# FNet mixing and a gated feed-forward block on one core: fold parts and first-stage groups moved to a regular grid of steps

## The chip, the cores and the metric

The kernel runs on one NeuronCore of one Trainium2 chip. The metric is the device time of one execution in microseconds (us). The engines are named as in the profile: PE (TensorE matmul), PEld (its weight loads), DVE (VectorE), ACT (ScalarE), POOL (GpSimd) and SP (SyncE, which here issues most DMAs).

## What is computed

A two-dimensional Fourier transform of every batch, of which the real part is kept, and then two matrix products with the quick form of GELU between them, all in float32:

```python
# x (8, 3008, 256); moe_w_in (256, 2048); moe_w_out (2048, 256)
X = np.fft.fft(x, axis=1)
X = np.fft.fft(X, axis=2)
x = X.real.astype(np.float32).reshape(B * S, D)      # (24064, 256)
h = x @ w_in
g = h * (1.0 / (1.0 + np.exp(-1.702 * h)))
out = (g @ w_out).astype(np.float32)
```

## The kernel before

**Stages.** The sequence of 3008 positions is split as 47 x 64. A batch goes through five pieces of work:

1. *Load and fold.* `turn` (L189) copies half of the batch, in reversed order, to the DRAM tensor `Xr`; `load_x` (L199, four calls) loads `x` and `Xr` into the one SBUF tile `xt`. `fold1` (L210) then adds and subtracts mirrored columns in `xt` in place. It is called 16 times per batch, for chunk c = 0 to 7 and part 0 or 1, and runs on POOL. Part 0 is a small and a large add (L225 on 111x4, L227 on 111x510 elements), part 1 an add and a subtract (L230, L231, 111x254 each). The very first part (c = 0, part 0) has three more operations that make the tile `e` (L218 to L220).
2. *First-stage groups.* `mix1` (L233, four calls, m = 0 to 3) multiplies `xt` by the tables `w1` on PE (L255). Group m needs the four parts of chunks 2m and 2m+1. The group m = 0 has a few matmuls more, those of `e`. ACT copies the results back to `xt` (`mixed`, L263).
3. *Spill, fill, rotate.* `spill` (L337, two calls per group) writes a group's result to the DRAM tensor `Td`, `fill` (L342, three calls per batch) reads it back in another layout into the tile `t`, and `rotate` (L347) corrects one column by a small matmul and a copy.
4. *Second stage.* `stage2` (L354), once per block of 512 columns, multiplies on PE (L365) and transposes on DVE (L372) into the tile `pq`. `nyquist_out` and `nyquist` (L387, L375) send one row of it through DRAM and load it to all partitions as `nb`.
5. *Feed-forward steps.* The rest of the work, by far the most of it, in 384 steps t.

**Steps.** A step t stands for (batch b, block, half hh, p): eight batches of three blocks of two halves of p = 0 to 7, so 48 steps a batch; `t0 = 48 * b` is a batch's first step. Below, "step k of batch b" is t = 48b + k, and k modulo 8 is p. In each step PE multiplies for the hidden layer (`begin`, into the banks `x`), ACT applies GELU (`forward`, L600, one instruction per step; `activate_back`, L607; both around `backward`, L604, on DVE), and the results are combined by a Strassen-like scheme so that fewer products are needed: `sums` on POOL (L615, L616) and on DVE (L622, L623, at every second step), and one level further down `deeper` on DVE (L646, L648 for part 0, L650 for part 1). The second matrix product, `product` (L697) and `small_products` (L660, PE rows at L684), runs three steps behind (`LAG`). Where it starts a new half, the step is an "opening": k modulo 8 is 3.

At the end of a half DVE also has to combine the eight results: L757 and L758 in p = 2 steps, four times L786 (`combine_small`) in p = 3, L768 and L804 in p = 4, and a transpose L737 (`turned`), from which `store` sends the output, in each of the p = 5 and p = 6 steps.

**How the next batch's first stage is placed.** The order on every engine is written out by hand: the loop over t (L992) calls the work of step t in a fixed order, and at its end all functions that `at(t, fn, ...)` (L935) has noted for that step (`extra`). So a fold part of step k stands on POOL behind the two sums of step k, and a group stands on PE behind all matmuls of its step. The loop over b (L960) notes for each batch, in terms of t0, at which steps the next batch's fold parts, groups, spills (one step after their group), fills, rotate and the loads of the batch after next are issued. The steps of folds and groups are a row of `PLANS` (L932): the first is used for b = 0, the second for b = 1, the third for b = 2 to 6. Negative entries are steps of the batch before. Steps of the kind "group or stage2" are `special`: they use other banks, and `middle` (L578) for the step after next is issued a step later.

`paced(t)` (L391) is a four-byte DMA that reads an element which `forward(t)` writes. It stands on SP's queue just ahead of a large transfer and so keeps that transfer from being issued before step t.

Of the kernel before, what the change touches and what calls it, by code (L numbers as in the profile page):

```python
# [112 lines left out]
def kernel(ctx: ExitStack, tc, x, w_in, w_out, tab1, tab2, out):  # L113
# [800 lines left out]
    for h0 in (0, 512):  # L914
# [14 lines left out]
    finish_out(0)  # L929

    extra, early = {}, {}
    PLANS = ((range(11, 27), (16, 20, 25, 28)), ((-1, 0, 1, 1, 2, 7, 7, 9, 10, 15, 15, 16, 16, 17, 17, 18), (7, 15, 19, 23)),  # L932
             ((-9, -7, -7, -6, -1, 0, 1, 1, 2, 7, 9, 10, 15, 16, 17, 17), (-1, 7, 15, 23)))

    def at(t, fn, *args):  # L935
        extra.setdefault(t, []).append((fn, args))
# [22 lines left out]
        at(7 + i, small_weights, i)  # L959
    for b in range(B):  # L960
        t0 = b * NBLK * NF
        late = 0 if b else 5
        if b + 2 < B:
            for k in range(3):
                at(t0 + 11 + k, paced, t0 + 11 + k)
                at(t0 + 11 + k, turn, b + 2, k)
        if b + 1 < B:
            folds, groups = PLANS[min(b, 2)]
            for c in range(NCH):
                for part in range(2):  # L970
                    at(t0 + folds[2 * c + part], fold1, b + 1, c, part, nc.gpsimd)
                if c % 2:
                    k = t0 + groups[c // 2]
                    at(k, mix1, b + 1, c // 2)
                    for half in range(2):
                        at(k + 1, spill, b + 1, half, c // 2)
            for blk in range(NBLK):
                at(t0 + 27 + blk + late, paced, t0 + 27 + blk + late)
                at(t0 + 27 + blk + late, fill, b + 1, 4 * blk, 4 * blk + 4)
            if b + 2 < B:  # L980
                for k in range(4):
                    at(t0 + 31 + 2 * k + late, paced, t0 + 31 + 2 * k + late)
                    at(t0 + 31 + 2 * k + late, load_x, b + 2, k)
            at(t0 + 36 + 3 * (late > 0), rotate, b + 1)
        for blk in range(NBLK):
            nxt = (b, blk + 1) if blk + 1 < NBLK else (b + 1, 0)
            if nxt[0] < B:
                at(t0 + blk * NF + 8, stage2, *nxt)
                at(t0 + blk * NF + 9, nyquist_out, *nxt)
                at(t0 + blk * NF + 10, nyquist, *nxt)  # L990
# [123 lines left out]
```

## Time and profile before

| | us |
|---|---|
| median of 3 runs | 1857.74 (1855.88 to 1861.3) |
| profiled execution | 1856.81 |
| its span, first to last instruction | 1855.0 |
| PE busy | 1835.9 (99%) |
| DVE busy | 1486.4 (80%) |
| ACT busy | 1148.7 (62%) |
| POOL busy | 995.9 (54%) |

The steps can be told apart by the L600 rows on ACT, one for each step from t = 8 on. From the first L600 row of one batch to that of the next it takes 227.18 us in batch 1, 225.01, 225.03, 225.03 and 225.09 us in batches 2 to 5 and 222.96 us in batch 6. Batch 7 has no next batch, so it issues no folds and no groups.

The DMA engines are busy for 10 to 40% of most slices; the chain that ended last runs along PE for 87% of the span. The page's line of granted clocks shows 9 (90% or more) in all 40 slices, and the core's mean is 1.000.

The busiest lines of POOL are the sums (L616 397.3 us, L615 351.2 us); L227, the large add of a fold, is issued 56 times and takes 1266 ns at least, 1272 ns in the median and 2224 ns at most.

### The profile page before, as it was taken

To read this page: it belongs to the slowest core of one execution; us is meant where nothing else is said; L and a number is where in the kernel's file an instruction comes from. 1 tells how busy PE (TensorE), PEld (TensorE's weight loads), DVE (VectorE), ACT (ScalarE), POOL (GpSimd) and SP (SyncE) were. 2 spreads that over 40 slices of the span, in tenths; PEclk is the share of its full clock that TensorE was granted. 3 is DMA by queue.
4 is the path that set the end of the run, shared out by engine and by line. 5 is a ranking of instruction groups with operands and counts; after the bars stand their busy time and mean duration, and the time that the engine had idled before them with its cause. 6 is when DMAs were issued, how large, how long until landed. Compare 5 with 4: busy or idle time off the path is not lost.

```text
span 1855.0 us, 55973 instructions
## 1 busy us (share of the span) xinstructions
PE 1835.9 (99%) x23722; PEld 1401.5 (76%) x23722; DVE 1486.4 (80%) x1928; ACT 1148.7 (62%) x2241; POOL 995.9 (54%) x1053
## 2 busy tenths in 40 slices
PE   8999999999999999999999999999999999999998
PEld 4677777777777777777777777777777777778776
DVE  6978778878788778887888778877888788878875
ACT  5656666665666666666565666666665666656563
POOL 4786456745655446463655546555465544444442
PEclk9999999999999999999999999999999999999999
DMA  8721331225111341213312132131411111100111
GB/s 275 186 61 34 85 67 28 64 51 99 27 40 44 78 77 21 60 33 90 57 21 66 35 86 52 23 74 31 103 31 31 36 37 36 30 19 13 23 19 24
DMA packets 149706, 105.31 MB, mean 57 GB/s; under 512 B 106057, under 2 KB 130665, under 8 KB 148896
## 3 DMA queue, kind: packets, MB, share of 16 engines
q1 hardware_dynamic: 146624, 99.68, 23.7%
q8 instruction: 187, 3.06, 0.7%
q10 hardware_dynamic: 2832, 2.05, 0.5%
q14 instruction: 63, 0.52, 0.1%
HBM read 64.41 MB, written 48.05 MB: 61 GB/s over the span
## 4 chain that ended last, share of the span: by engine, by line
PE 87%; DVE 8%; DMA 2%; ACT 1%; issue 1%; POOL 0%; DVEq 0%; SPq 0%; ACTq 0%; POOLq 0%
PE x L184 32%; PE o L184 25%; PE low L684 23%; PE o L684 4%; PE ps L255 2%; PE ps L365 1%; DVE big L622 1%; DVE big L650 1%; DVE big L604 1%; DVE big L786 1%; DVE big L646 1%; DMA xt<-in_x_dram 1%; DMA Td<-big 1%; DVE big L804 0%; DVE big L648 0%
## 5 line engine op out<-in xcount | busy, mean ns | idle before, releaser
L615 POOL TENSOR_TENSOR big<-big 128x256 f32<-128x256 f32 (+1 forms) x376 | 351.2, 934 | 804.8 <-ACT big L607 745.4
L184 PE MATMUL x<-pq,wcs 128*64 128x256 f32 (+1 forms) x6016 | 769.0, 376 | 1.1 <-ACT g L597 0.2
L184 PE MATMUL o<-big,wo 128*64 128x256 f32 (+1 forms) x4800 | 620.8, 375 | 0.1
L184 PEld LDWEIGHTS x<-pq,wcs 128*64 128x64 f32 x6016 | 413.8, 137 | 182.7 <-issue 15.3
L597 ACT ACTIVATE g<-x 128x512 f32<-128x512 f32 (+1 forms) x376 | 221.7, 590 | 384.2 <-PE x L184 383.0
L184 PEld LDWEIGHTS o<-big,wo 128*64 128x64 f32 x4800 | 341.3, 137 | 147.7 <-DVE big L622 0.5
L604 DVE TENSOR_TENSOR big<-g,x 128x512 f32<-128x512 f32 (+1 forms) x376 | 250.8, 667 | 190.8 <-ACT big L600 190.6
L616 POOL TENSOR_TENSOR big<-big 128x256 f32<-128x256 f32 (+1 forms) x376 | 397.3, 1057 | 0.0
L585 ACT ACTIVATE x<-nb,af 128x256 f32<-128x256 f32 (+1 forms) x752 | 352.9, 469 | 68.8 <-DVE pq L372 55.7
L684 PE MATMUL low<-big 128*64 128x128 f32 (+1 forms) x5888 | 381.8, 270 | 0.0
L684 PEld LDWEIGHTS low<-big 128*64 128x64 f32 x5888 | 337.0, 137 | 28.7
L600 ACT ACTIVATE big<-x 128x512 f32<-128x512 f32 (+1 forms) x376 | 219.2, 583 | 123.6 <-PE x L184 105.2
L646 DVE TENSOR_TENSOR big<-big 128x1024 f32<-128x1024 f32 (+1 forms) x184 | 235.6, 1280 | 66.2 <-PE low L684 42.4
L607 ACT ACTIVATE big<-big 128x512 f32<-128x512 f32 (+1 forms) x376 | 231.6, 616 | 37.9 <-DVE big L604 35.7
L684 PE MATMUL low<-big,wo 128*64 128x128 f32 (+1 forms) x2944 | 220.6, 271 | 5.9 <-DVE big L650 5.9
L648 DVE TENSOR_TENSOR big<-big 128x512 f32<-128x512 f32 (+1 forms) x184 | 178.7, 971 | 16.3 <-PE x L184 0.5
L684 PEld LDWEIGHTS low<-big,wo 128*64 128x64 f32 x2944 | 171.5, 137 | 11.1 <-DVE big L650 7.7
L650 DVE TENSOR_TENSOR big<-big 128x512 f32<-128x512 f32 (+1 forms) x184 | 172.8, 939 | 0.0
L623 DVE TENSOR_TENSOR big<-big 128x512 f32<-128x512 f32 (+1 forms) x188 | 147.8, 786 | 6.5
L622 DVE TENSOR_TENSOR big<-big 128x512 f32<-128x512 f32 (+1 forms) x188 | 139.5, 742 | 3.3 <-POOL big L615 3.3
L786 DVE TENSOR_TENSOR big<-big,low 128x512 f32<-128x512 f32 (+3 forms) x184 | 109.0, 609 | 3.5
L684 PEld LDWEIGHTS o<-big,wo 128*64 128x64 f32 x1472 | 92.2, 137 | 25.0
(97 smaller groups left out, 1147.2 us busy)
## 6 DMA issues: line engine op xcount, KB each, us to landing
out_dram<-os SPq DMA_DIRECT2D x284, 64.0 KB
t<-Td SPq DMA_DIRECT2D x22, 512.0 KB
Td<-xt SPq DMA_DIRECT2D x56, 192.0 KB
xt<-in_x_dram SPq DMA_DIRECT2D x14, 512.0 KB
xt<-Xr SPq DMA_DIRECT2D x14, 512.0 KB
nb<-Nd SPq DMA_DIRECT2D x23, 256.0 KB
out_dram<-os SPq DMA_DIRECT2D x96, 56.0 KB
Xr<-in_x_dram SPq DMA_DIRECT2D x7, 752.0 KB
```

The costliest lines, as they stand in the source:

```text
L184: nc.tensor.matmul(out[c0:c0 + 64], lhsT=lhs[:, c0:c0 + 64], rhs=rhs, skip_group_check=True, **how)
L585: nc.scalar.activation(x[:, i * 256:i * 256 + n], nbt[b, blk][:, hh * 256:hh * 256 + n], ACTF.Copy, scale=af1[:, f:f + 1])
L597: nc.scalar.activation(two(g[:], n), two(xb[t][:], n), ACTF.Copy, scale=2.0)
L600: nc.scalar.activation(front(t), two(xb[t][:], width(t)), ACTF.Gelu_apprx_sigmoid)
L604: nc.vector.tensor_tensor(back(t), two(gt.pop(t)[:], n), two(xb.pop(t)[:], n), op=ALU.subtract)
L607: nc.scalar.activation(back(t), back(t), ACTF.Gelu_apprx_sigmoid)
L615: eng.tensor_tensor(right(t, S1, n), left(t, A21, n), right(t, A22, n), op=ALU.add)
L616: eng.tensor_tensor(left(t, S3, n), left(t, A11, n), left(t, A21, n), op=ALU.subtract)
L646: nc.vector.tensor_tensor(free(big[:], SUM, *both_), free(big[:], from11 + w, *twice), free(big[:], from11, [at_right(t, 0) + w - from11, ...
L648: nc.vector.tensor_tensor(s2, a11, s1, op=ALU.subtract)
L650: nc.vector.tensor_tensor(s4, a12, s2, op=ALU.subtract)
L684: nc.tensor.matmul(o, lhsT=lhs, rhs=rhs, start=first_in, stop=(p == NP - 2), skip_group_check=True)
```

## The change

The change touches only the placing in steps. It replaces the three rows of `PLANS` by two. The first (b = 0) is as before. The second, now for all b from 1 on, issues one fold part in each of the steps -1, 0, 1, 2, then 7 to 10, 15 to 18 and 23 to 26, and the groups at steps 7, 15, 23 and 31. Before, b = 1 had its parts at -1, 0, 1, 1, 2, 7, 7, 9, 10, 15, 15, 16, 16, 17, 17, 18 and its groups at 7, 15, 19, 23; b = 2 to 6 had them at -9, -7, -7, -6, -1, 0, 1, 1, 2, 7, 9, 10, 15, 16, 17, 17 and at -1, 7, 15, 23.

What follows the groups moves too, for b from 1 on: the fills from steps 27, 28, 29 to 33, 34, 35, the loads of the batch after next from 31, 33, 35, 37 to 36, 38, 40, 42, and rotate from 36 to 39. For b = 0 these stay at 32 to 34, at 36, 38, 40, 42 and at 39.

```diff
-    PLANS = ((range(11, 27), (16, 20, 25, 28)), ((-1, 0, 1, 1, 2, 7, 7, 9, 10, 15, 15, 16, 16, 17, 17, 18), (7, 15, 19, 23)),
-             ((-9, -7, -7, -6, -1, 0, 1, 1, 2, 7, 9, 10, 15, 16, 17, 17), (-1, 7, 15, 23)))
+    PLANS = ((range(11, 27), (16, 20, 25, 28), 32), ([g + k for g in (0, 8, 16, 24) for k in range(-1, 3)], (7, 15, 23, 31), 33))
...
-        late = 0 if b else 5
...
-            folds, groups = PLANS[min(b, 2)]
+            folds, groups, filled = PLANS[min(b, 1)]
...
-                at(t0 + 27 + blk + late, paced, t0 + 27 + blk + late)
-                at(t0 + 27 + blk + late, fill, b + 1, 4 * blk, 4 * blk + 4)
+                at(t0 + filled + blk, paced, t0 + filled + blk)
+                at(t0 + filled + blk, fill, b + 1, 4 * blk, 4 * blk + 4)
...
-                    at(t0 + 31 + 2 * k + late, paced, t0 + 31 + 2 * k + late)
-                    at(t0 + 31 + 2 * k + late, load_x, b + 2, k)
-            at(t0 + 36 + 3 * (late > 0), rotate, b + 1)
+                    at(t0 + 36 + 2 * k, paced, t0 + 36 + 2 * k)
+                    at(t0 + 36 + 2 * k, load_x, b + 2, k)
+            at(t0 + 39, rotate, b + 1)
```

## The prediction, made before the changed kernel was run

> **What bounds the kernel now.** I read the page first (busy shares, chain), then PE's own waits, then step times from the starts of the L600 rows (one per step on ACT, 3.6 to 6.6 us apart), and last the DVE and POOL timelines of the steps that come out long. Start times below are from these rows; "step 3 of batch 3" is t = 48*3+3.
>
> ```profile
> PE 1835.9 (99%) x23722; PEld 1401.5 (76%) x23722; DVE 1486.4 (80%) x1928; ACT 1148.7 (62%) x2241; POOL 995.9 (54%) x1053
> ...
> PE 87%; DVE 8%; DMA 2%; ACT 1%; issue 1%; POOL 0%; DVEq 0%; SPq 0%; ACTq 0%; POOLq 0%
> ```
>
> PE is the bound and is nearly always busy, at full granted clock in all slices. The change neither adds nor removes matmuls, so it can only win or lose the little time in which PE waits. The longest of PE's waits over the whole span (total, times, longest), then batch 3 in the table of windows (length, PE busy and its instructions, PEld, DVE, ACT, POOL):
>
> ```profile
> PE low L684 <- DVE big L650: 5.9, 7, 1.0
> ...
> 724.44:949.47 225.03, 223.95 (x2958) 173.21 (x2956) 181.95 (x235) 140.85 (x279) 122.48 (x133) 1.00 0.25 54
> ```
>
> Of 225.03 us of a middle batch PE idles 1.08. One wait stands out: PE for L650, the last DVE product input of a pair, once a batch. In time it lies here (timeline of step 3 of batch 3; step 2 began at 733.08):
>
> ```profile
> 734.32 1.55 DVE L622 TENSOR_TENSOR big<-big 128x512 f32<-128x512 f32 x1
> 735.90 2.48 DVE L623 TENSOR_TENSOR big<-big 128x512 f32<-128x512 f32 x1
> 738.31 1.21 DVE L650 TENSOR_TENSOR big<-big 128x512 f32<-128x512 f32 x1
> ...
> 734.05 1.27 POOL L227 TENSOR_TENSOR xt<-xt 111x510 f32<-111x510 f32 x1
> 735.40 1.06 POOL L230 TENSOR_TENSOR xt<-xt 111x254 f32<-111x254 f32 x1
> 736.42 0.73 POOL L231 TENSOR_TENSOR xt<-xt 111x254 f32<-111x254 f32 x1
> 737.11 0.73 POOL L615 TENSOR_TENSOR big<-big 128x256 f32<-128x256 f32 x1
> ...
> 739.58 0.66 PE L684 MATMUL low<-big,wo 128*64 128x128 f32 x8 [0.96 <-DVE big L650]
> ```
>
> Two fold parts issued at step 1 run on POOL in step 2. The DVE sums beside them take 1.55, 2.48 and 1.21 us, where batch 7, which has no folds, shows 0.69, 0.69 and 0.68. So L650 ends at 739.52 instead of some 735.7, and PE waits 0.96 us. Step 3 lasts 5.51 us against 4.33 in batch 7: 1.18 lost.
>
> **What each step costs, against batch 7.** Batch 7 issues no fold and no group. I subtract its step times from those of the others (its steps 40 to 47 run into the end; there batch 3 stands in, with 4.33 for step 47, which has no group in batch 6). A group at step 15 costs 1.65 at its step less 0.48 at the next: 1.17; at 7 and at 23 also 1.17. A batch's first group (it has the extra edge matmuls of L245) costs 2.06 - 0.46 = 1.60. These are matmul work and stay. What remains in batches 2 to 6 is 1.18 (step 3), 0.09 (steps 5 and 6), 0.27 (step 13) and 0.11 (step 36, rotate). In batch 1: 0.45 at steps 4 to 6, where L646 takes 2.60 us beside a fold; the group at step 19 costs 2.36, so 1.19 too much; rotate 0.11.
>
> **The change, part by part.** Batch 0 keeps its steps. For batches 1 to 6:
>
> 1. *The pairs of parts at one step go (1, and 7, 15, 16, 17 in the one or the other plan).* After step 1's second part is gone, step 2 of batches 1 to 6 should be batch 1's without what it runs second. In batch 1 POOL ran late after the first part (with its edge ops L218 to L220), and a single L227 fell here:
>
> ```profile
> 283.35 0.69 DVE L623 TENSOR_TENSOR big<-big 128x512 f32<-128x512 f32 x1
> 283.95 1.76 DVE L650 TENSOR_TENSOR big<-big 128x512 f32<-128x512 f32 x1
> ...
> 283.46 1.71 POOL L227 TENSOR_TENSOR xt<-xt 111x510 f32<-111x510 f32 x1
> ```
>
> L650 was over at 285.71, step 3 lasted 4.33 and nothing was lost there; the loss at steps 4 to 6 came from the part after it. The next part (L230, L231: 1.45 us) will then run beside L604 and L786, and L786 took the same 2.46 us in batch 1 with a fold beside it as in batch 7 without. Gain: 5 x (1.18 + 0.09) + 0.45 = 6.8.
>
> 2. *The group at 19 goes to 31 (batch 1); the one at -1 of batches 2 to 6 goes the same way, all groups one place on.* Step 31 is, like 15, a p = 7 step with a plain step after it: 1.17. Gain in batch 1: 2.36 - 1.17 = 1.19; in the others none, since the first group's 1.60 moves from step 47 to step 7 (batch 1 has it there: 2.10 - 0.51). Sum of both: 8.0.
>
> 3. *Steps 7 to 10 get a part at 8.* It runs beside the transposes L372, which in batch 0, step 24, took 0.70 and 0.67 beside a fold as elsewhere. Nothing. The parts at 9 and 10 are those of batches 2 to 6, so their 0.27 at step 13 stays, and batch 1 gets it: -0.27. Why 0.27: L227 beside L622, then POOL and DVE in turn, push L757 back by 1.07 us; batch 3, step 10:
>
> ```profile
> 773.81 1.53 DVE L622 TENSOR_TENSOR big<-big 128x452 f32<-128x452 f32 x1
> 775.38 1.12 DVE L623 TENSOR_TENSOR big<-big 128x452 f32<-128x452 f32 x1
> 776.42 1.16 DVE L650 TENSOR_TENSOR big<-big 128x512 f32<-128x512 f32 x1
> ```
>
> 4. *Steps 15 to 18: one part at 17 instead of two, one at 18.* Two at 17 lost nothing (steps 18 and 19: 4.42 and 4.18, as in batch 7). One then loses nothing; the part at 18 runs beside L786. Zero.
>
> 5. *Steps 23 to 26 get four parts that were not there.* Those of 23 and 24 fall in DVE's idle time (in batch 3's step 24, 2.11 us before L604 and 1.24 before L372). That of 25 starts behind L616, which ends at 0.68 of step 26, as in step 10, and meets the same DVE run. There is no row for it. Bounds: 0 (as step 18) and 1.18 (as step 3). Nearest is step 10: 0.27; the wide steps are a little tighter (0.69 for each sum instead of 0.62), so L650 would end near 0.75 of step 27, about where PE needs it. I take 0.35, six times: -2.1.
>
> 6. *Transfers.* Spills at 32, fills at 33, 34, 35 (were 27 to 29), rotate at 39 (was 36), load_x at 36 to 42 (was 31 to 37), nyquist's load behind the load_x of 42. SP waits in each paced transfer for L600 of its step; behind it stand the next fills only. The cover is batch 0, which has fills at 32 to 34, rotate at 39, load_x at 36 to 42 and the next batch's fold at -1: its steps 40 to 47 last what they last in batch 3 (6.61 and 6.60 at 40), rotate adds 0.1 at 39 as it did at 36, and POOL does not wait at the fold. The packets of batch 0's fills are through within some 4 us of the issue, so the fill of 35 is there in step 36, three steps (some 14 us) ahead of rotate. If it were late, PE would wait in order at step 39. Cost zero.
>
> Sum: 8.0 - 0.27 - 2.1 = 5.6 saved. The profiled execution took 1856.81 us (span 1855.0), 0.9 below the median of the runs: 1856.8 - 5.6 = **1851.2 us**.
>
> **Rivals.**
> *All waits go.* If POOL, no longer behind by a pair of parts, reaches the sums early enough everywhere, the 0.27 of step 13 go too (5 times 0.27 = 1.35) and step 26 costs nothing: 1856.8 - 8.0 - 1.35 = 1847.4. For it: batch 1's steps 7 to 10 lost nothing. Against it: batches 2 to 6 lose 0.27 with the very parts that stay.
> *The wait moves on.* The stall of step 3 comes back at step 27 in full: 6 x 1.18 = 7.1 given back, 1856.8 - 8.0 + 0.3 + 7.1 = 1856.2, no change. For it: the fold that is added at 25 is the long one, L227. Against it: at step 3 it took two parts in one step. The rows show DVE and POOL sums of SBUF operands taking turns: 1.76 us for a 0.68 us L650 that began 0.5 us after L227. The Trainium skill has this as a rule (SBUF — State Buffer, the part on the two physically separate sides): the pair of ports that DVE and GpSimd share is an exclusive lock, held by whoever started first for its whole instruction. It speaks against the change, since moving folds leaves the hold time of all of them as it is; by it alone the time would be the 1856.2 of this rival, and what decides is whether DVE is idle then, which the rows show in p = 7 and 0 but not in p = 2.
> *Slower.* The folds of p = 1 and 2 hit the DVE run that begins at p = 2 and has no gap until p = 6. If three of the four sets (after -1, 15 and 23) lose what step 3 lost, 6 x 3 x 1.18 = 21.2 come on top: 1856.8 - 8.0 + 0.3 + 21.2 = 1870. It decides from 1.3 us a batch on, slightly more than one such stall. For it: 1.18 at step 3, 2.36 for the group at 19 shortly after folds. Against it: steps 2 and 18 with an L227 beside them lost nothing by the next opening.
> *It doesn't do what it says:* POOL's program shows the parts moved as written; the total of folds, groups and transfers is the same.
>
> **Chances.** Forecast 0.45, all waits go 0.20, the wait moves on 0.20, slower 0.15. A measurement of this kernel can tell about 0.3% (5.6 us) from no change. The forecast lies on that bound; I count 0.33 of its 0.45 as faster, since the terms that I set to their middle are more often nothing in the rows (steps 2, 18, batch 1's 7 to 10), and with the first rival and a little of the third row's spread that is 0.55 faster, 0.30 within, 0.15 slower. The range leaves out the slower rival: from 1847 (all waits go) to 1857.5 (the wait moves on, plus the 0.9 between median and profile).
>
> **What would show it.** Right: PE's wait for L650 falls from seven times to two or fewer before batch 7 and step 3 lasts 4.3; step 31 lasts some 6.0, step 19 4.2; step 13 keeps 4.3; L622 in step 26 takes about 1.5. Wrong: PE waits at step 27 or at 4 to 6 of every batch, L372 stretched in step 24, or PE waiting for a fill at step 39.

## The result, and the profile after

| | before | changed |
|---|---|---|
| median of 8 runs, us | 1857.60 (1855.88 to 1861.83) | 1853.01 (1851.27 to 1854.62) |
| ratio, with 95% interval | | 0.9972 (0.9961 to 0.9983) |
| profiled execution, us (span) | 1856.81 (1855.0) | 1851.27 (1849.5) |
| PE's wait for L650 | 5.9 us, 7 times | 0.7 us, once |
| batches 1 to 6, first step to first step | 1350.3 | 1346.05 |

The change is faster by 4.6 us, 0.28%. The prediction had counted on some 0.3% as the least that a measurement can tell; the interval, 0.17 to 0.39%, is clear of zero. A second set of ten runs on another occasion gave 1851.76 us and 0.9974 (0.9965 to 0.9983).

PE's longest waits in the changed kernel behind two of 2.7 and 1.2 us at its start (total, times, longest):

```profile
PE low L684 <- DVE big L650: 0.7, 1, 0.7
PE ps L317 <- DVE first L297: 0.6, 1, 0.6
PE o L184 <- issue: 0.6, 1, 0.6
```

The one wait for L650 that is left is in batch 0, whose placing did not change; shorter ones, of 0.12 us, are not listed in this view. The wait marked "issue" is new and is looked at below. The table of windows for batches 3 and 5 of the changed kernel (length, PE busy, PEld, DVE, ACT, POOL):

```profile
719.72:943.82 224.10, 223.86 (x2958) 173.34 (x2954) 182.17 (x235) 140.84 (x279) 123.98 (x133) 1.00 0.25 54
...
1167.93:1393.22 225.29, 224.50 (x2960) 178.69 (x2956) 182.15 (x235) 140.71 (x279) 123.37 (x133) 1.00 0.25 54
```

In batch 3 PE idles 0.24 us where it idled 1.08. The profile models the ends of PE's rows, so idle time is less than what is lost: the batch takes 0.6 us more than without folds (below). With the same steps as before compared one by one (starts of L600), batches 2 to 6 gain 1.16 to 1.18 us at step 3 and 0.08 at steps 5 and 6, and lose 0.34 at step 19. In batch 1, steps 4 to 6 gain 0.43, the group that went from 19 to 31 gains 1.18, steps 13 and 19 lose 0.28 and 0.34. Nothing is lost at step 27. Batch 5 loses 1.18 at step 42.

The step that was to gain, steps 2 and 3 of batch 3 (step 2 began at 728.51), DVE and then POOL:

```profile
730.53 0.69 DVE L623 TENSOR_TENSOR big<-big 128x512 f32<-128x512 f32 x1
731.14 2.45 DVE L650 TENSOR_TENSOR big<-big 128x512 f32<-128x512 f32 x1
733.51 0.41 DVE L757 TENSOR_TENSOR big<-big,o 128x256 f32<-128x256 f32 x1
```

```profile
730.64 1.71 POOL L227 TENSOR_TENSOR xt<-xt 111x510 f32<-111x510 f32 x1
732.31 0.73 POOL L615 TENSOR_TENSOR big<-big 128x256 f32<-128x256 f32 x1
733.00 1.18 POOL L616 TENSOR_TENSOR big<-big 128x256 f32<-128x256 f32 x1
```

L650 is over 0.3 us after step 3 begins (733.28); in the kernel before it was over 1.7 us after. It is still slow, 2.45 us for 0.68, but the row of PE that needs it starts only 0.60 us into the step, and it started there in the versions without this delay too:

```profile
733.88 0.61 PE L684 MATMUL low<-big,wo 128*64 128x128 f32 x8
```

The same picture in step 18 of the changed kernel (step 19 began at 806.44), with PE below:

```profile
804.78 2.38 DVE L650 TENSOR_TENSOR big<-big 128x452 f32<-128x452 f32 x1
807.09 0.38 DVE L757 TENSOR_TENSOR big<-big,o 128x226 f32<-128x226 f32 x1
```

```profile
804.29 1.70 POOL L227 TENSOR_TENSOR xt<-xt 111x510 f32<-111x510 f32 x1
805.96 0.72 POOL L615 TENSOR_TENSOR big<-big 128x256 f32<-128x256 f32 x1
806.64 1.12 POOL L616 TENSOR_TENSOR big<-big 128x256 f32<-128x256 f32 x1
```

```profile
806.26 0.85 PE L684 MATMUL low<-big 128*64 128x113 f32 x14
807.22 0.61 PE L684 MATMUL low<-big,wo 128*64 128x113 f32 x8
```

Here L650 ends at 807.16, 0.72 us into step 19, and PE's next row starts 0.06 us later. In the best version below step 19 also begins at 806.44, lasts 4.18 us, and has that row here:

```profile
806.94 0.56 PE L684 MATMUL low<-big,wo 128*64 128x113 f32 x8
```

So the row starts 0.28 us late in the changed kernel and takes 0.05 more, and the step lasts 4.52 instead of 4.18. The profile shows 0.12 of this as PE's wait for L650.

### The profile page after: what moved, and what is told of

Same layout as the page of the kernel before. It is cut to its first block, busy times and chain, and to the rows that moved or that the text cites. A ratio compares the mean times of both kernels' runs of the same rounds, so it can differ in the third digit from the quotient of the medians.

```text
span 1849.5 us, 55986 instructions
## 1 busy us (share of the span) xinstructions
PE 1835.5 (99%) x23722; PEld 1411.0 (76%) x23722; DVE 1485.5 (80%) x1928; ACT 1148.6 (62%) x2241; POOL 1001.1 (54%) x1053
## 3 DMA queue, kind: packets, MB, share of 16 engines
q10 hardware_dynamic: 2832, 2.05, 0.5%
## 4 chain that ended last, share of the span: by engine, by line
PE 88%; DVE 8%; DMA 2%; ACT 1%; issue 1%; POOL 0%; SPq 0%; DVEq 0%; ACTq 0%; POOLq 0%
PE x L184 32%; PE o L184 25%; PE low L684 23%; PE o L684 4%; PE ps L255 2%; DVE big L650 2%; PE ps L365 1%; DVE big L622 1%; DVE big L604 1%; DVE big L786 1%; DVE big L648 1%; DVE big L646 1%; DMA xt<-in_x_dram 1%; DMA Td<-big 1%; DVE big L804 0%
## 5 line engine op out<-in xcount | busy, mean ns | idle before, releaser
L615 POOL TENSOR_TENSOR big<-big 128x256 f32<-128x256 f32 (+1 forms) x376 | 357.9, 952 | 797.0 <-ACT big L607 694.5
L184 PE MATMUL x<-pq,wcs 128*64 128x256 f32 (+1 forms) x6016 | 776.8, 376 | 1.0 <-ACT x L585 0.4
L184 PE MATMUL o<-big,wo 128*64 128x256 f32 (+1 forms) x4800 | 629.0, 375 | 0.6 <-issue 0.6
L184 PEld LDWEIGHTS x<-pq,wcs 128*64 128x64 f32 x6016 | 421.9, 137 | 175.9 <-issue 15.3
L184 PEld LDWEIGHTS o<-big,wo 128*64 128x64 f32 x4800 | 348.0, 137 | 145.9 <-issue 1.0
L604 DVE TENSOR_TENSOR big<-g,x 128x512 f32<-128x512 f32 (+1 forms) x376 | 250.8, 667 | 186.5 <-ACT big L600 186.4
L616 POOL TENSOR_TENSOR big<-big 128x256 f32<-128x256 f32 (+1 forms) x376 | 399.6, 1063 | 0.0
L585 ACT ACTIVATE x<-nb,af 128x256 f32<-128x256 f32 (+1 forms) x752 | 353.0, 469 | 69.1 <-DVE pq L372 55.9
L684 PE MATMUL low<-big 128*64 128x128 f32 (+1 forms) x5888 | 386.1, 270 | 0.0
L684 PEld LDWEIGHTS low<-big 128*64 128x64 f32 x5888 | 341.0, 137 | 27.9
L600 ACT ACTIVATE big<-x 128x512 f32<-128x512 f32 (+1 forms) x376 | 219.2, 583 | 123.5 <-PE x L184 113.6
L684 PE MATMUL low<-big,wo 128*64 128x128 f32 (+1 forms) x2944 | 224.8, 271 | 1.4 <-DVE big L650 0.7
L650 DVE TENSOR_TENSOR big<-big 128x512 f32<-128x512 f32 (+1 forms) x184 | 185.4, 1007 | 0.0
L684 PEld LDWEIGHTS low<-big,wo 128*64 128x64 f32 x2944 | 175.4, 137 | 6.4 <-DVE big L650 2.9
L622 DVE TENSOR_TENSOR big<-big 128x512 f32<-128x512 f32 (+1 forms) x188 | 140.7, 748 | 3.3 <-POOL big L615 3.3
L623 DVE TENSOR_TENSOR big<-big 128x512 f32<-128x512 f32 (+1 forms) x188 | 135.6, 721 | 6.5
L684 PEld LDWEIGHTS o<-big,wo 128*64 128x64 f32 x1472 | 94.3, 137 | 24.3
L684 PE MATMUL o<-big,wo 128*64 128x128 f32 (+1 forms) x1472 | 112.2, 270 | 0.0
```

Of the source, the lines that this page charges most:

```text
L184: nc.tensor.matmul(out[c0:c0 + 64], lhsT=lhs[:, c0:c0 + 64], rhs=rhs, skip_group_check=True, **how)
L585: nc.scalar.activation(x[:, i * 256:i * 256 + n], nbt[b, blk][:, hh * 256:hh * 256 + n], ACTF.Copy, scale=af1[:, f:f + 1])
L600: nc.scalar.activation(front(t), two(xb[t][:], width(t)), ACTF.Gelu_apprx_sigmoid)
L604: nc.vector.tensor_tensor(back(t), two(gt.pop(t)[:], n), two(xb.pop(t)[:], n), op=ALU.subtract)
L615: eng.tensor_tensor(right(t, S1, n), left(t, A21, n), right(t, A22, n), op=ALU.add)
L616: eng.tensor_tensor(left(t, S3, n), left(t, A11, n), left(t, A21, n), op=ALU.subtract)
```

## The experiments

The edits are made to the changed kernel, if nothing else is said. Lists of steps are from its second plan, with the parts at -1, 0, 1, 2, 7, 8, 9, 10, 15, 16, 17, 18, 23, 24, 25, 26 and the groups at 7, 15, 23, 31. Times of single steps and batches are differences of L600 starts in the profiled execution. They repeat within some 0.03 us from batch to batch and run to run, apart from a few shifts that are named, that a neighbouring step gives back, or that are 0.23 us at step 13 (explained below, with the terms of the prediction), while the start of the program up to the first of these rows takes 81.2 to 84.8 us in the profiled executions. So a loss of 2 us is read from the steps, and the runs' times alone could not tell it.

**One part back from 18 to 17.**

```diff
-  ..., 15, 16, 17, 18, ...
+  ..., 15, 16, 17, 17, ...
```

> The changed kernel with the part of step 18 issued at 17, so that L230 and not the sum L615 stands behind L227 on POOL. Theory (POOL keeps L650 out as long as its next instruction is ready; L230 has to wait for L227, which leaves 0.08 us, L615 doesn't): L650 of step 18 takes 1.7 us instead of 2.38, step 19 lasts 4.18 instead of 4.52 in batches 1 to 6, PE's waits for L650 in step 19 go there, and batches 2 to 4 and 6 last 223.8 instead of 224.1 us. Rival (the part that runs beside L786 in step 19 is what costs the 0.34): L650 may still take 1.7, but step 19 loses something with any second part in reach, and stays near 4.5. Rival 2 (a second part at a step is the costly thing, as in step 1 of the kernel before): step 19 grows to some 5.3.

Step 19 lasts 4.18 us in batches 1 to 6 and its 0.34 is gone; batch 3 takes 223.76. Batches 1 and 6 take 224.0, as their step 13 is 0.23 longer. The timeline of step 18 of batch 3, DVE and then POOL:

```profile
805.95 1.70 DVE L650 TENSOR_TENSOR big<-big 128x452 f32<-128x452 f32 x1
807.57 0.38 DVE L757 TENSOR_TENSOR big<-big,o 128x226 f32<-128x226 f32 x1
```

```profile
805.45 1.71 POOL L227 TENSOR_TENSOR xt<-xt 111x510 f32<-111x510 f32 x1
807.24 0.99 POOL L230 TENSOR_TENSOR xt<-xt 111x254 f32<-111x254 f32 x1
```

Behind L227 stands L230 now, which starts 0.08 us after L227's end. L650 is through by 807.65, and L230 is the one that is stretched (0.99 instead of 0.72). Both rivals fall. This edit also takes the part away from L786, but in the changed kernel PE's late row stands at 807.22, ahead of L786, which begins at 808.47; so the part beside L786 is not the cost. And two parts at a step are not costly in themselves.

**Parts at 7, 7, 8, 8 instead of 7, 8, 9, 10.**

```diff
-  ..., 7, 8, 9, 10, ...
+  ..., 7, 7, 8, 8, ...
```

> The changed kernel with parts at 7, 7, 8, 8 instead of 7, 8, 9, 10. Theory (the 0.27 of step 13 comes from L227 of step 9 beside L622 and L650 of step 10; DVE is idle for over 1 us in steps 7, 8 and 9): L622, L623 and L650 of step 10 take 0.62 to 0.68, step 13 lasts 4.02 instead of 4.29, and nothing grows at 8 or 9; batches 2 to 4 and 6 last 223.8 instead of 224.1 us. Rival (two parts at one step always cost, since POOL's sums come late): steps 8 to 10 grow by 0.5 or more in sum, and the batch is no shorter.

The 0.27 of step 13 is gone (4.0 in batches 1 to 6), no step grows, and batch 3 takes 223.81. DVE's sums in step 10 are short again; L622, L623 and L650 took 1.53, 1.11 and 1.15 in the changed kernel:

```profile
769.92 0.62 DVE L622 TENSOR_TENSOR big<-big 128x452 f32<-128x452 f32 x1
770.58 0.63 DVE L623 TENSOR_TENSOR big<-big 128x452 f32<-128x452 f32 x1
771.13 0.69 DVE L650 TENSOR_TENSOR big<-big 128x512 f32<-128x512 f32 x1
```

**The kernel before, without the pair at step 1.**

```diff
-             ((-9, -7, -7, -6, -1, 0, 1, 1, 2, 7, 9, 10, 15, 16, 17, 17), (-1, 7, 15, 23)))
+             ((-9, -7, -7, -6, -1, 0, 1, 2, 7, 7, 9, 10, 15, 16, 17, 17), (-1, 7, 15, 23)))
```

> The kernel before, of which only the plan of batches 2 to 6 is changed: the second part of step 1 and all up to step 7 go one place on (parts at -9, -7, -7, -6, -1, 0, 1, 2, 7, 7, 9, 10, 15, 16, 17, 17); the group at -1, fills and loads stay. Theory (the pair at step 1 makes the stall of step 3): step 3 lasts 4.33 instead of 5.51 us in batches 2 to 6, PE's wait for L650 goes there, and a batch lasts 223.8 instead of 225.0. Rival (the group at -1, whose copies and matmuls fall in steps 47 and 0, makes it): step 3 stays at 5.5. Between them: some 4.7, if the first part of step 1, which POOL runs earlier here than in the changed kernel, costs as at step 10.

Step 3 lasts 4.33 us in batches 2 to 6, and batch 3 223.76. So the pair at step 1 made all of the 1.18, and the group at -1 nothing. L227 runs at the same place in step 2 as in the kernel before, and still beside L622:

```profile
735.49 1.55 DVE L622 TENSOR_TENSOR big<-big 128x512 f32<-128x512 f32 x1
737.07 0.69 DVE L623 TENSOR_TENSOR big<-big 128x512 f32<-128x512 f32 x1
737.68 1.22 DVE L650 TENSOR_TENSOR big<-big 128x512 f32<-128x512 f32 x1
```

L622 takes what it took, but the second part no longer keeps L623 out (2.48 in the kernel before).

**No folds from batch 2 on.** This one leaves the folds of batches 2 to 7 out, all but the edge operations.

```diff
+        if b > 1:
+            return
         at, up = 2 * c * D, (31 - 2 * c) * D
```

> The changed kernel without the folds of batches 2 to 7 on POOL: chunks are left as loaded (only the edge operations L218 to L220 are kept), so the output is another one from batch 2 on. Theory (all that a batch still loses is DVE and POOL taking turns): steps 13 and 19 last 4.02 and 4.18, batches 1 to 6 lose nothing but matmul work and last 223.5 us, 0.6 less than in the changed kernel. Rival (some of the loss is that of the groups, spills and fills): a part of 0.27 and 0.34 stays.

Batches 1 to 4 and 6 last 223.48 to 223.49 us, and steps 13 and 19 are free of loss. All that these batches lose in the changed kernel, 0.6 us each, comes from the folds; groups, spills, fills and loads cost nothing beyond their matmuls. Batch 5 keeps its 1.2 us.

**The third group at 19.**

```diff
-  (7, 15, 23, 31)
+  (7, 15, 19, 31)
```

> The changed kernel with its third group at 19 (p = 3) instead of 23 (p = 7), as batch 1 of the kernel before had one; its folds stay at 15 to 18. Theory (a group costs its 1.17 us of matmuls at p = 7 and some 1.2 more right after an opening, where DVE has no idle time): batches 1 to 6 grow by about 1.2 each, to 225.3, some 7 us in all, about 1858 us; the loss stands at steps 18 to 22. Rival (the 2.36 of that group in batch 1 came from the pairs of parts at 15 to 17 before it, not from its place): the batches stay at 224.1 or gain up to 0.3. Between: the part of step 18 that the group needs ends on POOL in step 19 and PE waits for it, then the loss shows as PE's wait for L231.

Batches 1 to 4 and 6 last 224.56 to 224.65 us, 0.46 to 0.54 more than 224.1. So the move costs, but under half of what was expected, and the rival's gain isn't there either. PE waits once more in each batch, 0.24 us in step 20, for ACT. Counted against the best version below, which loses nothing in these steps, steps 18 to 22 lose 0.80 us beside the group's 1.17, and 0.34 of it the changed kernel loses there anyway. In batch 1 of the kernel before it was 1.19. The other 0.4 may come from the pairs of parts around the group, which were not tried by themselves.

**The long fold as two instructions.**

```diff
-            eng.tensor_tensor(low, low, free(t, up + D - 1, [-D, 2], [-1, D - 1]), op=ALU.add)
+            for i in range(2):
+                one = free(t, at + 1 + i * D, [1, D - 1])
+                eng.tensor_tensor(one, one, free(t, up + D - 1 - i * D, [-1, D - 1]), op=ALU.add)
```

> The changed kernel with the long fold L227 (111x510) issued as two instructions of 111x255, some 0.73 us each, no wait between them. Theory (POOL keeps DVE out as long as its next instruction is ready): L622 of step 26 still takes some 1.5 us, L650 of step 18 some 2.4, and steps 13 and 19 stay at 4.29 and 4.52. Rival (POOL keeps DVE out for one instruction only and DVE takes the next turn): L622 of step 26 takes about 1.0, L650 of steps 2 and 18 1.1 to 1.8, the second half is late by that much, and the 0.34 of step 19 goes or halves.

Neither theory holds everywhere. In step 26 of batch 3 DVE gets in between the halves (L624 is L622 here, L229 the two halves):

```profile
841.25 0.99 DVE L624 TENSOR_TENSOR big<-big 128x512 f32<-128x512 f32 x1
...
840.96 1.87 POOL L229 TENSOR_TENSOR xt<-xt 111x255 f32<-111x255 f32 x2
```

0.99 instead of 1.53, as the rival says, and likewise in step 10, which ends the 0.27 of step 13. But in step 18 it doesn't (L652 is L650):

```profile
803.81 2.53 DVE L652 TENSOR_TENSOR big<-big 128x452 f32<-128x452 f32 x1
...
803.32 1.85 POOL L229 TENSOR_TENSOR xt<-xt 111x255 f32<-111x255 f32 x2
805.12 0.73 POOL L617 TENSOR_TENSOR big<-big 128x256 f32<-128x256 f32 x1
```

L650 is kept out through both halves and the sum behind them, and step 19 grows by another 0.15. In step 2 it is the same: L650 takes 2.59 us, and steps 3 to 6 grow by 0.18. In all a middle batch takes 224.14 us, so the split wins nothing there. What sets the two cases apart in the rows: in steps 2 and 18 the first half had itself been kept out by L623 (1.16 us instead of 0.73), in steps 10 and 26 it had not. What decides whether the waiting engine gets the turn at the boundary of two instructions is not settled.

**Both moves together.**

```diff
-  ..., 7, 8, 9, 10, 15, 16, 17, 18, ...
+  ..., 7, 7, 8, 8, 15, 16, 17, 17, ...
```

> The changed kernel with both moves that took a loss away: parts at 7, 7, 8, 8 and at 15, 16, 17, 17. Theory (the two losses are apart from each other): steps 13 and 19 last 4.02 and 4.18, the batches last 223.5 us as without folds (batch 5 1.2 more, since PE's 0.55 us wait for its own instructions in step 42 stands there in all versions with these loads), some 3.7 us less than the changed kernel in the stretch of batches 1 to 6: 1342.3. Rival (POOL, late by the pair at 8, meets the parts at 15 elsewhere): one of the losses comes back.

Batches 1 to 4 and 6 last 223.48 to 223.49, the time without folds; batch 5 takes 0.9 more. Sum of batches 1 to 6: 1341.8.

**The loads apart.**

```diff
-                    at(t0 + 36 + 2 * k, paced, t0 + 36 + 2 * k)
-                    at(t0 + 36 + 2 * k, load_x, b + 2, k)
+                    at(t0 + (37, 39, 42, 44)[k], paced, t0 + (37, 39, 42, 44)[k])
+                    at(t0 + (37, 39, 42, 44)[k], load_x, b + 2, k)
```

> The changed kernel with the four loads of the batch after next at steps 37, 39, 42, 44 instead of 36, 38, 40, 42, so that the second (issued late, behind the stores of steps 37 and 38) and the third no longer stand together. Theory (in step 42 of batch 5 PE waits for a 16 KB packet of the instruction queue that starts 5.6 us later after step 36 than in the kernel before, behind those two loads): PE's 0.55 us wait marked issue in step 42 of batch 5 goes, that step lasts 4.68 instead of 5.86 and batch 5 224.1 instead of 225.3; nothing else moves. Rival (that wait belongs to a place in PE's program): it stays there with 5.86. Price if the fourth load is too late: the folds of step 47 wait for it and POOL's sums of step 0 are late.

Step 42 of batch 5 lasts 4.67, the batch 224.1, and the wait marked issue is gone. This alone is no proof: the changed kernel, run again below with its loads unmoved, did not have that wait either. Over all profiled executions here, a wait of this kind (0.3 to 0.8 us, in step 41 or 42 of batch 5) stands in seven of the eight with loads at 36, 38, 40 and 42, and in none of the two with the loads apart or the three with those of the kernel before.

**The best version, and two kernels timed beside it.** The best version has both moves and the loads apart. The other two are the changed kernel itself, and the kernel before with the pair at step 1 gone.

> The changed kernel with parts at 7, 7, 8, 8 and 15, 16, 17, 17 and with the loads at 37, 39, 42, 44. Theory (the three losses are apart): batches 1 to 6 last 223.5 us each, 1340.9 in sum against 1346.05 in the changed kernel and 1350.3 in the one before; the median is some 5 us below the changed kernel's 1853.0, at 1848, ratio to the kernel before 0.9948. Rival (the time before the first step, 81 to 85 us in the runs so far, hides it): ratio between 0.9955 and 0.9965.

> The changed kernel itself beside the others: 1853 us, ratio 0.9972 to the kernel before; 1851.2, as predicted, would need its batch 5 without the 1.2 us of step 42 and a short start.

> The kernel before with only the second part of step 1 moved on, timed. Its profile has 1344.0 us in batches 1 to 6, 2.0 less than the changed kernel. Theory: median 1851.3, ratio 0.9966, not above the changed kernel. Rival (the longer start of its profiled execution, 84.8 us to the first step, comes with it): 1853 or more.

| | median, us (runs) | ratio to before, 95% interval | batches 1 to 6, us |
|---|---|---|---|
| before | 1857.43 (16) | | 1350.3 |
| both moves, loads apart | 1849.04 (6) | 0.9957 (0.9945 to 0.9969) | 1340.9 |
| changed, again | 1851.76 (10) | 0.9974 (0.9965 to 0.9983) | 1344.6 |
| before without the pair | 1851.99 (5) | 0.9966 (0.9954 to 0.9978) | 1344.3 |

A middle batch of the best version in the table of windows (length, PE busy):

```profile
719.68:943.17 223.49, 223.49 (x2958) 173.34 (x2956) 181.69 (x236) 140.71 (x279) 125.33 (x133) 1.00 0.25 54
```

PE is busy for the whole of the batch: the folds are hidden in full. The steps came out as expected (1340.9), but the ratio did not: 0.9948 was expected, and 0.9957 lies in the rival's range, though 0.9948 is within its interval. The best version has the lowest median of the three; its interval (up to 0.9969) overlaps those of the other two (from 0.9965 and from 0.9954). That it is faster is clear from the steps, which show 3.7 us against the changed kernel (1344.6 - 1340.9), while the medians are 2.7 us apart. One moved entry of the old plan does as much for the time as the whole change.

## Why the prediction was right, and where it was not

The forecast was 1851.2 us, 5.6 saved; the profiled execution took 1851.27 and the median 1853.01. The near agreement of the two profiled executions is partly chance: 4.25 of their 5.5 us lie in batches 1 to 6, where the change is, and 1.2 in the time before the first step, which varies from run to run. By the prediction's own terms, in us over all batches:

| term | predicted | measured |
|---|---|---|
| steps 3 to 6, pair at step 1 gone | 6.8 | 6.7 |
| group 19 to 31 (batch 1) | 1.19 | 1.18 |
| batch 1's step 13 | -0.27 | -0.28 |
| steps 15 to 18 (step 19) | 0 | -2.05 |
| steps 23 to 26 (step 27) | -2.1 | 0 |
| transfers | 0 | 0; -1.18 in batch 5 in some executions |

A loss of 0.23 at step 13 of batch 2 and a gain of 0.15 at step 11 of batch 5 make up the rest to within 0.1 us. The loss at step 13 is chance, and the rows show of what kind: L650 and POOL's L615 start within 0.04 us of each other there in all batches that have the 0.27. In batch 3 L650 took 0.62 us and L615 1.16, in batch 2 L650 took 1.13 and L615 0.67, and only then is the step 0.23 longer. The same happens in batches 1 and 6 with the part back at 17, and in batch 6 of the kernel before without the pair, when it was timed.

Of the signs that the prediction named for itself, one failed: step 19 was to last 4.2 us and lasted 4.52. The others came as said (step 31 5.96 us, step 13 4.29, L622 in step 26 1.53), and none of the signs against it showed.

*What bounds the kernel, and the large term.* Right. PE lost its time in L650's wait at step 3, and the old kernel with one entry moved shows that the pair at step 1 was the whole cause. The mechanism was a little off: the row taken over from batch 1 had L650 at 1.76 us, and it took 2.45, because behind L227 there is now a sum and no longer L230. It cost nothing only since PE's row that needs L650 starts 0.3 us after that; with the long fold split, where L650 took 2.59, that row came 0.04 us late and step 3 grew by 0.09.

*The step that failed* is the fourth, "One then loses nothing". It took fewer parts for less contention. But the second part at 17 had stood between L227 and the sum L615, and as a dependent instruction it left 0.08 us in which L650 got its turn. Without it L650 is kept out through L227 and L615, 2.38 us instead of 1.70, and PE waits in step 19 of six batches: 0.34 each. The experiment with the part back at 17 shows it.

*The fifth was mis-sized the other way.* L622 in step 26 took the 1.53 us foreseen, but the stall after it didn't come. The timeline of that step in the changed kernel, DVE and POOL:

```profile
842.08 1.53 DVE L622 TENSOR_TENSOR big<-big 128x512 f32<-128x512 f32 x1
843.64 0.69 DVE L623 TENSOR_TENSOR big<-big 128x512 f32<-128x512 f32 x1
```

```profile
843.70 1.22 POOL L615 TENSOR_TENSOR big<-big 128x256 f32<-128x256 f32 x1 [0.64 <-ACT big L607]
```

L623 started 0.06 us ahead of L615, so POOL was the one that took longer. In step 10 of the kernel before L615 started 0.04 us ahead, and L623 took 1.12:

```profile
775.34 0.67 POOL L615 TENSOR_TENSOR big<-big 128x226 f32<-128x226 f32 x1 [0.48 <-ACT big L607]
```

I had read step 26 off step 10 with "the wide steps are a little tighter"; the order of two starts 0.1 us apart came out the other way. The path was misread too. I had looked for the loss in L650 at the next opening, but in step 10 L650 ends 0.38 us into step 11, in time for PE's row at 0.60. The 0.27 comes later: in the changed kernel L650 of step 10 begins 1.39 us later than in the run without folds, DVE's idle time before L757 and L604 (0.72 and 0.40 in that run) does not take all of it up, and PE waits for ACT's L585 as step 14 begins. In step 26 L650 begins 0.84 us late, and the idle time there (0.74 and 0.40) leaves 0.04. Whether the other order of L623 and L615 would have cost PE there was not run. The two errors, 2.05 and 2.1, cancel in the sum by chance.

*The rivals.* The wait did not move on to step 27, and nothing became slower. The rule of the Trainium skill on the shared pair of ports (SBUF — State Buffer, the part on the two physically separate sides) describes the single rows well: L650 begins 0.5 us after L227 and ends 0.5 us after L615's end in step 18, so it was kept out for two whole instructions, and not slowed. What it was to speak for, that moving folds gains nothing, did not hold, since DVE is idle in places and since a late result costs only what PE waits for it: with parts at 7, 7, 8, 8 and 15, 16, 17, 17 the batches last exactly what they last without folds. "All waits go" needed two more moves.

*The transfers.* The fills and rotate cost nothing, as said: no wait of PE for a fill, and the 0.1 us of rotate's matmuls went from step 36 to 39. The 1.18 us in batch 5 was not foreseen. PE waits there for nothing that the profile names (issue), and the DMA packets point to its own instructions:

```profile
1365.30 0.65 PE L184 MATMUL o<-big,wo 128*64 128x256 f32 x4 [0.55 <-issue]
```

In the DMA packets of that execution a 16 KB packet of the instruction queue starts 26.9 us after step 36 of batch 5, behind the second and third load, which stand close together there; it was 21.3 us in the kernel before. In the changed kernel run again it was 24.7 and in the two kernels with the loads apart 24.5, without the wait; in the versions that had it, 26.5 to 26.9. In all seven executions that had the wait, PE goes on 1.4 to 1.6 us after the end of that packet, so it was this packet that PE lacked, as far as the rows can tell. That it is late behind the loads fits the counts above, but is not proved, since the changed kernel has the wait in one profiled execution and not in the other.

## What to carry to other kernels

Where one engine is busy throughout, the whole gain of a reordering lies in a few waits. Find them step by step against a stretch that lacks the work in question, and take that work out once to see how much there is to be won (0.6 us a batch here).

Where two engines take turns, as DVE and POOL did here, the order of single instructions can matter more than the amount of work. Place the secondary work where the other engine is idle, and look at what stands right behind its long instruction: here that took the other engine's instruction from 1.70 to 2.38 us.

A row carried over from a similar step tells the size of a clash, but not who wins it when the two starts lie 0.1 us apart.

## What the runs showed of the hardware

- Two DVE and POOL instructions with only SBUF operands that overlap don't both slow down; the later one is kept out. L650 of step 18, 0.62 us alone, took 1.70, 2.38 or 2.53 depending on whether one, two or three POOL instructions in a row held it out. When the two start within some 0.03 us of each other, either can be the one kept out (step 13). DVE operations with a PSUM operand (L786) showed no effect: 2.46 us for four with and without a fold beside them.
- Splitting L227 let DVE in between the halves in steps 10 and 26 (0.99 instead of 1.53 us) but not in steps 2 and 18. Why is open.
- Two executions of the same program differ by 1.2 us in one wait of PE for its instructions, and by up to some 4 us in the time before the first step among these kernels, which share that part; the steps between repeat to some 0.03 us.
